# Attention in slots of six score steps instead of three, with GpSimd's queue in written order

## The chip, the cores and the metric

The kernel runs on one core of a Trainium2 chip. The metric is the device time of one execution in microseconds (us). Before the change the median of four runs is 950.72 us (950.05 to 951.18). PE is the matrix engine, DVE the vector engine, ACT the scalar engine, POOL is GpSimd, and SP is the engine that issues most DMAs here. SBUF is the on-chip memory, PSUM the banks into which the matrix engine writes.

## What is computed

Two blocks follow each other. The first is attention with a routing mask for 4 batches, 8 heads, 768 positions and 64 channels per head; a query sees only the keys whose nearest centroid (of 16 per head) is its own:

```python
mask = q_assign[:, :, :, None] == k_assign[:, :, None, :]
scores = scale * np.matmul(q, k.transpose(0, 1, 3, 2))
scores = np.where(mask, scores, -1000000000.0)
attn = np.exp(scores - np.max(scores, axis=-1, keepdims=True))
attn = attn / (np.sum(attn, axis=-1, keepdims=True) + 1e-09)
out = np.matmul(attn, v)
```

`q_assign` and `k_assign` are the argmax over the centroids of the normalized products. The second block takes the heads side by side as rows of 512, normalizes each row by its mean and variance, multiplies by `g_ln`, and adds `relu(xn @ w_ch1) @ w_ch2` (hidden width 2048) to the row. All is float32.

## The kernel before

**Tiling.** Two heads make a pair, so there are 16 pairs, numbered from 0. A pair is worked in two halves (384 queries each), and a half in six steps (128 keys each). One step (`scores`, line 380) is four groups of matmuls into one PSUM tile of two banks: the mask (two bf16 matmuls, one for each head) and the products of keys and queries (float32), and then one exp on ACT that writes a tile `e` of 128x768. There are three such PSUM tiles (`ps_s`), eight buffers for `e`, and one bank each for the sums (`ps_a`) and for everything else (`ps_t`). `weigh` (line 401) multiplies `e` by v on PE into the bank of `ps_a`, and DVE adds the `e` tiles of a half up into `es` for the denominators (lines 422 and 425, five additions a half). After the sixth step of a half ACT copies the sums into the tile `x` (line 434); `x` has two buffers, and a pair uses one.

**Preparation of the pair ahead.** `prep_transpose` turns q and k, either on PE in two groups of three with a copy on ACT each, or on DVE (line 280) when the load is in blocks of 32 columns. k of all pairs from 1 on is loaded in blocks, q of pair 1 and of the pairs from 7 on. `prep_sims` (295), `prep_turn` (314) and `prep_route` (323) find the nearest centroid, `prep_onehot` and `prep_mask` (339, 356) write three mask tiles on ACT.

**Finishing the pair behind** (`finish`, line 438). Part 0: the denominators by matmuls with ones (`den_ps`), a copy on ACT (`dsb`), and two small DMAs on POOL's queue, out to memory and back in another layout (`flat`, `rdens`). Part 1: a reciprocal on DVE (line 460) and three DMAs on POOL's queue (`row`, and two halves of `rb`). Part 2: `x` times `rb` on DVE (line 477) and a store. Part 3: a transpose on DVE (line 486) and four stores. Parts 0 and 1 of pair n-1 and parts 2 and 3 of pair n-2 run during pair n.

**Weights.** The weights come as 64-bit floats and are converted by six DVE instructions per chunk (`split_weight`, `join_weight`, lines 239 to 268), followed by a DMA on POOL's queue that adds the low part. The next chunk's load (line 236) goes out on SP when the one buffer is free. Pairs 0 to 6 convert two chunks, the later ones one.

**Work for the second block** of batch 0 is put into late pairs by `put` (lines 586 to 602): the row statistics (`norm_rows`, `norm_stats`, with a square root on ACT at line 524), `norm_stat_rows` (line 529: a transpose on PE, a copy on ACT, a store of 6 KB and two loads that spread mean and deviation over all partitions) and `norm_apply` (line 542), which subtracts and scales on DVE.

**Order.** The main loop (line 655) runs over four slots of three steps in each pair. In a slot PE computes the scores of the three steps after those that it weighs. PE, DVE and ACT execute in the order in which the loop writes their instructions; the order on SP and POOL is found by a planner. The second block (from line 721) gets its PSUM banks when the attention's pools are closed.

Of the kernel before, what the change touches and what calls it, by code (L numbers as in the profile page):

```python
# [8 lines left out]
F32 = mybir.dt.float32  # L9
# [10 lines left out]
def kernel(  # L20
# [11 lines left out]
    nc = tc.nc  # L32
# [37 lines left out]
    def ps(name, dt=F32, n=512):  # L70
        return pools["t"].tile([P, n], dt, tag="t", name=name)
# [201 lines left out]
    def prep_transpose(n, side, halves=range(NHALF)):  # L273
        src = loaded[n]["qk"[side]]
        if 0 in halves:
            prepared[n][side] = heads.tile([P, S], F32, tag=f"t{side}", name=f"t{side}")
        t_sb = prepared[n][side]
        if (n, "qk"[side]) in blocks:
            if 0 in halves:
                nc.vector.transpose(t_sb, src)  # L280
            return
        for g in halves:
# [7 lines left out]
            if n or side == 0 or g == 1:  # L290
# [147 lines left out]
    def finish(n, part):  # L438
        b, pr = pairs[n]
        if part == 0:  # L440
            den = ps("den_ps")
            for j in range(2):
                for g in range(NHALF):
                    r = (j * NHALF + g) * Q
                    nc.tensor.matmul(  # L445
                        den[r : r + Q, :HC], ones, sums[n, g][:, j, :],
                        start=True, stop=True, tile_position=(0, r),
                    )
            if n + 1 < len(pairs):
                dsb = last.tile([P, HC], F32, tag="dsb", name="dsb", bufs=1)  # L450
            else:
                dsb = late["all"][:, 1, :HC]
            nc.scalar.copy(dsb, den[:, :HC])
            flat = dram.tile([P // Q, HC], F32, tag="flat", name="flat")
            nc.gpsimd.dma_start(out=flat, in_=dsb[0:P:Q, :])
            nc.gpsimd.dma_start(
                out=rdens[:, n, :], in_=flat.rearrange("i (p e) -> (i p) e", e=DE)
            )
        elif part == 1:
            nc.vector.reciprocal(rdens[:, n, :], rdens[:, n, :])  # L460
# [13 lines left out]
            late[n] = rb  # L474
        elif part == 2:
            a, x = xs.pop(n), late[n]
            nc.vector.tensor_tensor(x, a, x, ALU.mult)
            nc.sync.dma_start(out=xT_d[b][pr], in_=x)
        else:
            x = late.pop(n)  # L480

            if n + 1 < len(pairs):
                y = last.tile([P, S], F32, tag="y", name="y")
            else:
                y = late["all"][:, 0]
# [41 lines left out]
        normed[b][1] = stat  # L527

    def norm_stat_rows(b):
        sp = ps("stat_ps")  # L530
        nc.tensor.transpose(
            sp[: 2 * NT, :P], normed[b][1].rearrange("p s t -> p (s t)"), ident
        )
        st = small.tile([2 * NT, P], F32, tag="st", name="st")
        nc.scalar.copy(st, sp[: 2 * NT, :P])
        nc.sync.dma_start(out=stat_d[b].rearrange("s (t p) -> (s t) p", p=P), in_=st)
        for i in range(2):
            row = xpool.tile([P, S], F32, tag="row", name="stat_row", bufs=2)
            nc.sync.dma_start(out=row, in_=stat_d[b][i : i + 1, :].to_broadcast([P, S]))
            normed[b].append(row)  # L540
# [51 lines left out]
    put(6, 2, rows_load, 0, 0)  # L592
# [7 lines left out]
    put(14, 1, x_sum, 0, 1)  # L600
    put(14, 3, x_sum, 0, 2)
    put(15, 2, w1_sums, 0, 0, (0, 1))


    steps = [(n, g, c) for n in range(len(pairs)) for g in range(NHALF) for c in range(NT)]
    per = NHALF * NT
    GROUP = 3
    slots = per // GROUP

    convert = {}  # L610
    for n in range(len(pairs)):
        for slot in (0, 2) if n < TWICE else (0,):
            convert[n, slot] = len(convert)
    order = {mybir.EngineType.PE, mybir.EngineType.DVE, mybir.EngineType.Activation}
    limit[0] = len(convert)
    with tc.manual_schedule(engines=order | {mybir.EngineType.SP}):
# [26 lines left out]
        prep_onehot(0)  # L643
        prep_mask(0, 0)
        prep_mask(0, 1)
        for i in range(1, GROUP):
            scores(i, "qk", ("qk",))
        for i in range(GROUP):
            scores(i, "qk", ("mask", "exp"))
        load_weight(0)  # L650
        for side in (1, 0):
            prep_transpose(1, side)
            load(2, "qk"[side])
    with tc.manual_schedule(engines=order):
        for u in range(len(pairs) * slots):
            n, slot = divmod(u, slots)
            nxt = n + 1 < len(pairs)
            if slot == 1:
                load(n + 1, "v")
            if slot == 1 and n > 1:  # L660
                finish(n - 2, 2)
            if slot == 1 and nxt:
                prep_sims(n + 1)
            if slot == 2 and nxt:
                prep_onehot(n + 1)
                prep_mask(n + 1, 0)
                prep_mask(n + 1, 1)
            if slot == 3 and n + 2 < len(pairs):
                prep_transpose(n + 2, 1)
                load(n + 3, "k")  # L670
                prep_transpose(n + 2, 0, (0,))
            for i in range(GROUP * (u + 1), min(GROUP * (u + 2), len(steps))):
                scores(i)
            if slot == 0 and n:
                finish(n - 1, 0)
            if slot == 1 and nxt:
                prep_turn(n + 1)
                prep_route(n + 1)
            if slot == 3 and n + 2 < len(pairs):
                prep_transpose(n + 2, 0, (1,))  # L680
                load(n + 3, "q")
            if slot == 1 and n > 1:
                finish(n - 2, 3)
            for i in range(GROUP * u, GROUP * (u + 1)):
                weigh(i)
            if slot == (2 if nxt else 1) and n:
                finish(n - 1, 1)
            if slot == 3 and not nxt:
                finish(n - 1, 2)
                finish(n - 1, 3)  # L690
# [479 lines left out]
```

## Time and profile before

| | us |
|---|---|
| median of four runs | 950.72 |
| the profiled execution's own time | 951.99 |
| its span | 950.2 |
| PE busy | 933.2 |
| DVE busy | 614.5 |
| ACT busy | 346.8 |
| POOL busy | 78.4 |

The attention fills about the first 361 us. The page of the profile gives the busy time of each engine, in tenths for 40 slices of the span, and groups of instructions by line with their mean duration and the idle time before them. The timeline gives single instructions with their start; what stands in brackets is the idle time of the engine before it and what ended it. A wait on an engine matters only where PE, or something that PE needs next, stands behind it.

### The profile page before, as it was taken

Reading aid. Unit: us, or ns where it says so; the run is one execution under the profiler, and the core shown is the slowest. Engines: PE = TensorE matmul, PEld = TensorE weight load, DVE = VectorE, ACT = ScalarE, POOL = GpSimd, SP = SyncE. Lnnn points to the kernel's source line nnn. Section 1 sums busy time; section 2 is a strip of 40 time slices with the busy share of each in tenths; the row PEclk is TensorE's granted clock in tenths of the full one; section 3 lists DMA queues with packets and bytes.
Section 4 is the critical chain, followed back from the end, with each engine's and each line's share of the span. In section 5 each row is a group of like instructions: output and inputs, shape, how many; then the busy total and the mean of one; then the engine's idle time right before and its main releaser. Section 6 shows DMA issues by size and latency. Waiting matters only on the chain.

```text
span 950.2 us, 12597 instructions
## 1 busy us (share of the span) xinstructions
PE 933.2 (98%) x4664; PEld 582.4 (61%) x4664; DVE 614.5 (65%) x1106; ACT 346.8 (36%) x554; POOL 78.4 (8%) x147
## 2 busy tenths in 40 slices
PE   8999999899999999999999999999999999999997
PEld 5444443344444444557887557887556887556886
DVE  5888888798999887898882446362436472344431
ACT  4667765477776762332001332001342000333000
POOL 2112111111111211110000000000000000000000
PEclk9999999999999999999999999999999999999999
DMA  6668898797798453664451002021002121000011
GB/s 141 150 150 196 190 195 182 158 193 159 173 166 147 112 132 99 147 140 141 140 155 39 0 1 78 22 95 40 1 0 65 36 84 50 1 1 7 29 45 36
DMA packets 179780, 92.48 MB, mean 97 GB/s; under 512 B 145792, under 2 KB 162288, under 8 KB 179712
## 3 DMA queue, kind: packets, MB, share of 16 engines
q1 hardware_dynamic: 170368, 76.20, 33.0%
q0 software_dynamic: 7744, 15.02, 8.0%
q8 instruction: 38, 0.62, 0.3%
q10 hardware_dynamic: 1600, 0.39, 0.2%
q14 instruction: 30, 0.25, 0.1%
HBM read 64.10 MB, written 19.10 MB: 88 GB/s over the span
## 4 chain that ended last, share of the span: by engine, by line
PE 83%; issue 7%; DVE 5%; DMA 2%; POOL 2%; ACT 0%; ACTq 0%; DVEq 0%; POOLq 0%
PE x_ps L831 17%; PE x_ps L738 16%; PE s_ps L396 11%; PE a_ps L408 9%; PE z_ps L831 9%; PE z_ps L738 8%; PE y_ps L831 4%; PE y_ps L738 4%; DMA row<-rdens 1%; DVE es L425 1%; PE sim_ps L302 1%; PE den_ps L445 1%; POOL w L268 1%; PE simT_ps L318 1%; PE oh_ps L344 1%
## 5 line engine op out<-in xcount | busy, mean ns | idle before, releaser
L391 ACT ACTIVATE e<-s_ps 128x768 f32<-128x768 f32 x192 | 150.2, 811 | 29.0 <-PE s_ps L396 24.1
L396 PE MATMUL s_ps<-t,t 64*128 64x384 f32 x768 | 155.2, 483 | 0.0
L408 PE MATMUL a_ps<-e,v_sb 128*64 128x384 f32 x768 | 138.8, 497 | 0.0
L425 DVE TENSOR_TENSOR es<-es,e 128x768 f32<-128x768 f32 x128 | 121.5, 949 | 10.7 <-ACT e L391 0.5
L408 PEld LDWEIGHTS a_ps<-e,v_sb 128*64 128x64 f32 x768 | 49.8, 137 | 75.4 <-issue 61.3
L758 DVE TENSOR_TENSOR h<-z_ps,u 128x384 f32<-128x384 f32 x64 | 35.6, 556 | 92.7 <-PE z_ps L738 71.3
L396 PEld LDWEIGHTS s_ps<-t,t 64*128 64x128 f32 x768 | 68.3, 188 | 28.6 <-issue 28.1
L831 PE MATMUL x_ps<-w2t,h 128*128 128x256 f32 x384 | 84.5, 379 | 0.0
L766 ACT ACTIVATE h<-h 128x384 f32<-128x384 f32 x96 | 49.9, 524 | 89.3 <-DVE h L758 89.3
L831 PEld LDWEIGHTS x_ps<-w2t,h 128*128 128x128 f32 x384 | 72.7, 190 | 10.1
L396 PE MATMUL s_ps<-m,mask 64*128 64x384 bf16 x192 | 62.4, 326 | 0.6 <-ACT e L391 0.6
L396 PE MATMUL s_ps<-mask,m 64*128 64x384 bf16 x192 | 62.2, 326 | 0.4 <-DVE mask L367 0.4
L753 ACT COPY u<-x_ps 128x384 f32<-128x384 f32 x64 | 30.7, 479 | 77.5 <-PE x_ps L738 77.5
L842 DVE TENSOR_TENSOR o_sb<-x_ps,xb 128x256 f32<-128x256 f32 x48 | 20.2, 420 | 50.4 <-PE x_ps L831 47.3
L753 ACT COPY p<-x_ps 128x384 f32<-128x384 f32 x32 | 15.0, 468 | 100.9 <-PE x_ps L738 97.4
L738 PE MATMUL x_ps<-xt,ws 128*128 128x384 f32 x128 | 46.7, 487 | 1.9 <-ACT p L753 1.1
L738 PE MATMUL x_ps<-xn,w 128*128 128x384 f32 x128 | 46.6, 487 | 0.6 <-ACT late L434 0.6
L738 PE MATMUL x_ps<-xn,ws 128*128 128x384 f32 x128 | 46.6, 487 | 0.2 <-DVE xn L567 0.2
L738 PE MATMUL z_ps<-xt,ws 128*128 128x384 f32 x128 | 46.6, 487 | 0.0
L738 PE MATMUL z_ps<-xn,ws 128*128 128x384 f32 x128 | 46.5, 486 | 0.0
L738 PE MATMUL x_ps<-xt,w 128*128 128x384 f32 x128 | 46.5, 486 | 0.0
L738 PE MATMUL y_ps<-xn,w 128*128 128x384 f32 x128 | 46.5, 486 | 0.0
(143 smaller groups left out, 1357.9 us busy)
## 6 DMA issues: line engine op xcount, KB each, us to landing
raw<-in_moe_w_ch_dram SPq DMA_DIRECT2D x32, 512.0 KB, 4.4
w<-tb POOLq DMA_DIRECT2D x32, 256.0 KB, 6.4
v_sb<-in_v_dram SPq DMA_DIRECT2D x32, 192.0 KB, 5.0
xn<-xT_d SPq DMA_DIRECT2D x16, 384.0 KB, 5.5
xr<-x_d SPq DMA_DIRECT2D x24, 256.0 KB, 3.1
xb<-x_d SPq DMA_DIRECT2D x48, 128.0 KB, 2.1
out_dram<-o_sb SPq DMA_DIRECT2D x48, 128.0 KB, 1.7
k_sb<-in_k_dram SPq DMA_DIRECT2D x62, 96.0 KB, 4.4
```

Source lines behind the costliest of these rows:

```text
L268: nc.gpsimd.dma_start(out=w, in_=fb, accum_op=ALU.add)
L302: nc.tensor.matmul(sim[r : r + Q, :HC], cT[:, pr, :, :].rearrange("p j c -> p (j c)"), prepared[n][side][:, g * HC : (g + 1) * HC], start= ...
L391: nc.scalar.activation(e, s[:, :, :HC], AF.Exp, scale=SCALE)
L396: nc.tensor.matmul(s[:, j, :HC], of_keys[:, keys], of_queries[:, cols], start=part == first, stop=part != first, skip_group_check=True,)
L408: nc.tensor.matmul(acc[j * D : (j + 1) * D, :HC], loaded[n]["v"][:, j, c, :], e[:, j, :], start=(c == 0), stop=(c == NT - 1),)
L425: nc.vector.tensor_tensor(es, es, soft.pop(i), ALU.add)
L738: nc.tensor.matmul(bank[:, :HC], lhs[:, c, :], rhs[:, c, :], start=first and c == 0, stop=c == NDH - 1, skip_group_check=True,)
L753: nc.scalar.copy(t, bank[:, :HC])
L758: nc.vector.tensor_tensor(h, bank[:, :HC], other, ALU.add)
L766: nc.scalar.activation(h, h, AF.Relu)
L831: nc.tensor.matmul(bank[:, :MH], hidden[lhs + (c,)][:, tt * P : (tt + 1) * P], rhs[:, c, :], start=first and c == 0, stop=c == NFH - 1, sk ...
L842: nc.vector.tensor_tensor(o, bank[:, :MH], x, ALU.add)
```

## The change

A slot now holds six steps, that is a half, and a pair has two slots. In a slot PE computes the scores of this half (`own`; the first three steps of pair 0 are done beforehand, `AHEAD`), then preparation, and then the products with v of the same half. Between scores and products stand `finish(n-1, 0)` and `prep_sims(n+1)` in slot 0, and `prep_onehot`, `prep_mask` and the PE transposes of q in slot 1. The transposes of q use a `ps_s` tile, six at a time with one copy; the denominators use the bank of `ps_a`. The conversion of a chunk is written before the half's `weigh`, in both slots of pairs 0 to 6 and in slot 0 of the later ones. After `weigh` come, in slot 0, `finish(n-2, 2)` and `(n-2, 3)` and the routing of pair n+1, and in slot 1 `finish(n-1, 1)` and the DVE transposes of k and q. The `put` jobs move to the two slots; `norm_stat_rows` goes into a new place between scores and products of slot 1 of pair 10. POOL's instructions keep the written order too. In pair 15 `finish(14, 0)` is written ahead of the scores, and `finish(15, 0)` ahead of the second block's first products.

```diff
@@ prep_transpose
+        if n:
+            t = ps_s.tile([P, 2, 512], F32, tag="s", name="qk_ps")
+            for c in range(NT):
+                nc.tensor.transpose(
...
+            nc.scalar.copy(t_sb.rearrange("p (g c) -> p g c", g=NHALF), t[:, :, :HC])
+            return
         for g in halves:
-            t = ps("qk_ps") if n else ps_s.tile([P, 2, 512], F32, tag="s", name="qk_ps")[:, 0]
+            t = ps_s.tile([P, 2, 512], F32, tag="s", name="qk_ps")[:, 0]
...
@@ finish, part 0
-            den = ps("den_ps")
+            den = ps_a.tile([P, 512], F32, tag="a", name="den_ps") if n + 1 < len(pairs) else ps("den_ps")
...
@@ norm_stat_rows
-        sp = ps("stat_ps")
+        sp = ps("stat_ps") if b else ps_s.tile([P, 2, 512], F32, tag="s", name="stat_ps")[:, 0]
...
-        put(7 + t // 2, (0, 2)[t % 2], norm_rows, 0, t)
-    put(9, 2, norm_stats, 0)
-    put(9, 3, norm_stat_rows, 0)
+        put(7 + t // 2, t % 2, norm_rows, 0, t)
+    put(9, 1, norm_stats, 0)
+    put(10, "between", norm_stat_rows, 0)
     for i in range(2):
         for c in range(NDC):
-            put(10 + 2 * i + c // 2, 2, norm_apply, 0, i, c)
+            put(10 + 2 * i + c // 2, 1 if i == 0 else c % 2, norm_apply, 0, i, c)
...
-    GROUP = 3
+    GROUP = NT
+    AHEAD = 3
...
-    with tc.manual_schedule(engines=order):
+    with tc.manual_schedule(engines=order | {mybir.EngineType.Pool}):
...
+            own = range(GROUP * u, GROUP * (u + 1))
+            if slot == 0 and not nxt:
+                finish(n - 1, 0)
+            for i in own:
+                if i >= AHEAD:
+                    scores(i)
+            if slot == 0:
+                if n and nxt:
+                    finish(n - 1, 0)
+                if nxt:
+                    prep_sims(n + 1)
+            elif nxt:
                 prep_onehot(n + 1)
                 prep_mask(n + 1, 0)
                 prep_mask(n + 1, 1)
...
+                if n + 2 < len(pairs) and (n + 2, "q") not in blocks:
+                    prep_transpose(n + 2, 0)
+                    load(n + 3, "q")
+            for job in extra.pop((n, "between"), ()) if slot else ():
+                job()
             if (n, slot) in convert:
                 m = convert[n, slot]
                 split_weight(m)
                 join_weight(m)
                 load_weight(m + 1)
+            for i in own:
+                weigh(i)
+            if slot == 0:
+                load(n + 1, "v")
+                if n > 1:
+                    finish(n - 2, 2)
+                    finish(n - 2, 3)
+                if nxt:
+                    prep_turn(n + 1)
+                    prep_route(n + 1)
+                else:
+                    finish(n - 1, 1)
+            elif not nxt:
+                for part in (2, 3):
+                    finish(n - 1, part)
+            else:
+                if n:
+                    finish(n - 1, 1)
+                if n + 2 < len(pairs):
+                    for side in (1, 0):
+                        if (n + 2, "qk"[side]) in blocks:
+                            prep_transpose(n + 2, side)
+                            load(n + 3, "qk"[side])
             for job in extra.pop((n, slot), ()):
                 job()
...
     with tc.manual_schedule(engines=order):
+        finish(len(pairs) - 1, 0)
         first_layer(0, 0, 1)
         first_layer(0, 0, 2)
         first_layer(0, 0, 6)
-        finish(len(pairs) - 1, 0)
```

More of the change, by code (lines that the diff above doesn't have):

```diff
@@ L281, in prep_transpose @@
             return
+        if n:
+            t = ps_s.tile([P, 2, 512], F32, tag="s", name="qk_ps")
+            for c in range(NT):
+                nc.tensor.transpose(
+                    t[:, c // TH, c % TH * P : (c % TH + 1) * P],
+                    src[:, c, :, :].rearrange("p h d -> p (h d)"),
+                    ident,
+                )
+            nc.scalar.copy(t_sb.rearrange("p (g c) -> p g c", g=NHALF), t[:, :, :HC])
+            return
         for g in halves:
-            t = ps("qk_ps") if n else ps_s.tile([P, 2, 512], F32, tag="s", name="qk_ps")[:, 0]
+            t = ps_s.tile([P, 2, 512], F32, tag="s", name="qk_ps")[:, 0]
             for c in range(TH):
@@ L289, in prep_transpose @@
                 )
-            if n or side == 0 or g == 1:
+            if side == 0 or g == 1:
                 nc.scalar.copy(t_sb[:, g * HC : (g + 1) * HC], t[:, :HC])
@@ L591 @@
     put(6, 0, norm_load, 0)
-    put(6, 2, rows_load, 0, 0)
+    put(6, 1, rows_load, 0, 0)
     for t in range(NT):
-        put(7 + t // 2, (0, 2)[t % 2], norm_rows, 0, t)
-    put(9, 2, norm_stats, 0)
-    put(9, 3, norm_stat_rows, 0)
+        put(7 + t // 2, t % 2, norm_rows, 0, t)
+    put(9, 1, norm_stats, 0)
+    put(10, "between", norm_stat_rows, 0)
     for i in range(2):
         for c in range(NDC):
-            put(10 + 2 * i + c // 2, 2, norm_apply, 0, i, c)
-    put(14, 1, x_sum, 0, 1)
-    put(14, 3, x_sum, 0, 2)
-    put(15, 2, w1_sums, 0, 0, (0, 1))
+            put(10 + 2 * i + c // 2, 1 if i == 0 else c % 2, norm_apply, 0, i, c)
+    put(14, 0, x_sum, 0, 1)
+    put(14, 1, x_sum, 0, 2)
+    put(15, 1, w1_sums, 0, 0, (0, 1))
     steps = [(n, g, c) for n in range(len(pairs)) for g in range(NHALF) for c in range(NT)]
     per = NHALF * NT
-    GROUP = 3
+    GROUP = NT
+    AHEAD = 3
     slots = per // GROUP
@@ L611 @@
     for n in range(len(pairs)):
-        for slot in (0, 2) if n < TWICE else (0,):
+        for slot in (0, 1) if n < TWICE else (0,):
             convert[n, slot] = len(convert)
@@ L645 @@
         prep_mask(0, 1)
-        for i in range(1, GROUP):
+        for i in range(1, AHEAD):
             scores(i, "qk", ("qk",))
-        for i in range(GROUP):
+        for i in range(AHEAD):
             scores(i, "qk", ("mask", "exp"))
@@ L657 @@
             nxt = n + 1 < len(pairs)
[L658 to L664, printed above, removed]
+            own = range(GROUP * u, GROUP * (u + 1))
[10 more added lines that the diff above has]
+            elif nxt:
                 prep_onehot(n + 1)
@@ L667 @@
                 prep_mask(n + 1, 1)
[L668 to L690, printed above, removed]
+                if n + 2 < len(pairs) and (n + 2, "q") not in blocks:
[3 more added lines that the diff above has]
+                job()
             if (n, slot) in convert:
```

## The prediction

> **What bounds the kernel now.** I read the page's slices first, then the timeline of PE, and then DVE, ACT and SP at the places where PE waits.
>
> ```profile
> PE   8999999899999999999999999999999999999997
> DVE  5888888798999887898882446362436472344431
> ```
>
> PE is busy nearly everywhere, so a gain must shorten PE's own sequence or remove one of its few waits. In the attention (the first 15 slices or so) DVE is close behind. The timeline of PE, at the last pair:
>
> ```profile
> 352.16 2.16 PE L408 MATMUL a_ps<-e,v_sb 128*64 128x384 f32 x12
> 354.25 0.33 PE L396 MATMUL s_ps<-m,mask 64*128 64x384 bf16 x1
> ...
> 355.07 0.32 PE L396 MATMUL s_ps<-m,mask 64*128 64x384 bf16 x1
> ...
> 355.87 0.32 PE L396 MATMUL s_ps<-m,mask 64*128 64x384 bf16 x1
> ...
> 356.77 4.09 PE L408 MATMUL a_ps<-e,v_sb 128*64 128x384 f32 x24
> 361.44 1.56 PE L738 MATMUL x_ps<-xn,w 128*128 128x384 f32 x4 [0.58 <-ACT late L434]
> 362.84 1.45 PE L738 MATMUL y_ps<-xn,w 128*128 128x384 f32 x4
> 365.36 1.56 PE L738 MATMUL x_ps<-xt,ws 128*128 128x384 f32 x4 [1.07 <-ACT p L753]
> ```
>
> Starts give what a group costs PE. A score step takes 0.82 or 0.80, the third 0.90 because the kind changes behind it; three steps 2.52. Three steps of products take 2.09 (352.16 to 354.25). Two such groups in a row, seen here only at the end, last 4.09, not 2.09 + 2.16. PE's waits in the attention are these:
>
> ```profile
> 151.54 0.85 PE L445 MATMUL den_ps<-es,ones 128*32 128x384 f32 x6 [2.33 <-DVE es L425]
> ...
> 177.39 1.50 PE L445 MATMUL den_ps<-es,ones 128*32 128x384 f32 x6 [4.08 <-DVE es L425]
> 178.82 3.14 PE L408 MATMUL a_ps<-e,v_sb 128*64 128x384 f32 x12
> ```
>
> The denominators of pairs 5 and 6 wait for DVE's additions, and DVE had waited for a small DMA:
>
> ```profile
> 143.28 0.23 DVE L460 RECIPROCAL rdens<-rdens 128x12 f32<-128x12 f32 x1 [2.14 <-DMA rdens<-flat]
> ...
> 169.13 0.23 DVE L460 RECIPROCAL rdens<-rdens 128x12 f32<-128x12 f32 x1 [3.89 <-DMA rdens<-flat]
> ```
>
> After the longer wait PE runs slower for a while (1.50 for six instead of 0.85 for eight, 3.14 instead of 2.16).
>
> **What the change takes away.** (a) 31 joints between score groups at 0.90 - 0.81 = 0.09 and 31 between product groups at 4.25 - 4.09 = 0.16: 7.7. (b) Five times two groups of three transposes of q become one of six: about 0.1 each, 0.5. (c) The waits above. From one pair's first denominator matmul to the next it is 20.94 in undisturbed pairs, and 21.50, 24.10 and 27.49 in pairs 5, 6 and 7: 10.3 too much. In POOL's old order `flat` stood behind a weight DMA that waited for DVE (issued 157.60 after 157.03, long after `dsb`); in written order it goes first. (d) At the end, 1.07 and 0.19 for an `rb` that landed late: now a half earlier, 1.3. Sum 19.8.
>
> **The new order, laid out.** Let T be the time from a pair's first score matmul. PE without waits: six scores to 4.97, denominators 0.78, similarities 0.79, six products 4.02 (to 10.56), turn 0.48, six scores from 11.04 to 16.01, one-hot 0.44, six products to 20.47; 0.87 more where q is turned on PE. The first exp starts 1.03 after the first score and takes 0.81. With three score tiles, the fourth score step (T = 13.49 in slot 1) needs the first exp's end.
>
> DVE, with a lag L behind the pair's start: conversion 3.31, five additions 4.89, so the product with `rb` (0.95) ends at L + 9.15; transpose 0.9, routing 1.08 (needs the turn, T = 11.1); in slot 1 conversion 3.31, additions 4.89, reciprocal 0.2, k and q 0.9 each. That is 20.5 for pairs 1 to 4, where PE needs 21.3, and 21.4 for pairs 5 and 6, where PE needs 20.5.
>
> Here is a new wait. Before, the product with `rb` was written ahead of ACT's copy of the first half's sums into `x`, 268.8 against 271.85. Now it is written behind, and `x` has two buffers, so the copy of pair n waits for the product of pair n-2. All exps of slot 1 stand behind that copy on ACT, and PE's fourth score step behind the first exp: L + 9.15 + 0.1 + 0.48 + 0.81 = L + 10.6 against 13.49. PE loses L - 2.9 whenever L is above 2.9.
>
> **What it adds.**
> - Pairs 5 to 8. L is near 0.1 to 1 up to pair 4. From then q too is loaded in blocks; SP needs 8.6 to 10.2 for the eight block loads (147.69 to 156.34; 124.45 to 134.72), and the next chunk's raw load, which must land for slot 1's conversion at T = 12.3, goes out behind them and takes 4.4. It lands 12.4 to 14.4. So pairs 5 and 6 add 0.9 of work each and 0 to 2 of waiting: L is 2.5 to 4.3 at pair 6 and 4.3 to 5.7 at pair 7, PE loses 0 to 1.4 and 1.4 to 2.8. I take 3.0. Bounds: nothing, if the loads are quick; 9, if `rb` lands in 8.5, its longest, not in its median 4.4.
> - The square root after pair 9.
>
> ```profile
> 235.53 1.28 ACT L524 ACT_TABLE_LOAD   x1
> 236.82 0.30 ACT L524 ACTIVATE stat<-mv,eps 128x6 f32<-128x6 f32 x1
> 237.14 1.28 ACT L391 ACT_TABLE_LOAD   x1
> ...
> 240.88 0.25 ACT L535 COPY st<-stat_ps 12x128 f32<-12x128 f32 x1
> ```
>
> These take 2.9 from 235.53 to 238.43, hidden before by the three steps that PE had in hand. Now they start when the pair's last sums are copied (T = 21.1), the first exp ends at 24.8 and PE wanted it at 22.9: 1.9. Bounds 0 and 2.9.
> - The row statistics in pair 10. `norm_stat_rows` moves from the end of pair 9 to slot 1 of pair 10, and the first `norm_apply` stays in that slot: DVE meets it about 10 us sooner. On ACT the copy `st` stands behind three masks (3.0) and ends 0.5 before the products do. SP then:
>
> ```profile
> 238.34 2.90 SPq L86 DMA_DIRECT2D k_sb<-in_k_dram  x4
> 241.34 2.71 SPq L86 DMA_DIRECT2D q_sb<-in_q_dram  x4
> 244.15 0.62 SPq L536 DMA_DIRECT2D stat_d<-st  x1
> ...
> 248.21 0.86 SPq L539 DMA_DIRECT2D stat_row<-stat_d  x2
> ```
>
> Before, the store left 3.0 after `st` (241.13), behind k and q, and the same loads stand there now. In a later batch with a free queue store to load is 2.4 (617.68 to 620.11), and the rows land 4.5 after issue. I take 3.0 + 2.4 + 4.5 = 9.9; then two subtractions of 0.9, less the 0.5: L = 11.2 at pair 11, and PE loses 8.3, plus 1.8 for the slow stretch after a long idle (1.50 - 0.64 and 3.14 - 2.16 above): 10.1. Bounds: free queue, 6.0 from copy to first subtraction (617.66 to 623.65), 6.2 in all; old spacing 7.1 and the longest landing 7.7, 15.
> - Pair 15: the denominators of pair 14 come first and wait for the bank's copy, 0.1 + 0.48 + 0.07 = 0.65.
> - Starting: similarities of pair 1 come 2 us earlier than before, and DVE's transposes may be late: 0.3 (0 to 2).
> - Each slot 0: products wait for `dsb`, ready at 6.4 to 6.5 against 6.54; 0.05 times 14 = 0.7 (0 to 1.5).
>
> POOL: `flat` goes at T = 6.5 and lands in 4.4, `rdens` follows and lands in 3.0, so at about 15 for a reciprocal at 20.5; by the longest rows (7.8 and 7.6) at 22.6, 2 late. The weight DMA behind them waits some 6 us longer; its buffer is next needed half a pair after it lands. The w additions of slot 1 now precede `row`, which costs `rb` about 1.
>
> Sum of what is added: 3.0 + 1.9 + 10.1 + 0.65 + 0.3 + 0.7 = 16.7. Against 19.8 that leaves -3.1 on the profiled execution's own 951.99 (span 950.2 and 1.8 around it), which stands 1.3 above the median: 947.6 on the median's scale.
>
> Two rules of the Trainium skill would move single terms. "DMA: Bandwidth & Descriptors", Latency and other measured facts, gives a fixed cost of about 2 us per DMA; by it the two DMAs of the row statistics would take 4 us instead of 9.9 and the estimate would be near 940, but even the trace's free queue shows 6.0. "ScalarE: Activation LUTs", What ACT_TABLE_LOAD costs, gives 2.66 us for each switch of table sets, 5.3 for two; by it the wait at the square root would be 4.6 and the estimate 950.3, but the trace's pair of loads with the square root between took 2.9.
>
> **Rivals.**
> - Short waits. If statistics arrive as with a free queue (6.2) and pairs 5 to 8 lose 1: 19.8 - 10.8 = 9.0, so 941.7. For it: the planner may put the store ahead of k and q. Against: `st` ends after DVE has released k and q.
> - DVE's lag feeds on itself (slower). Place: the product with `rb` in front of ACT's copy, from pair 2 on. DVE has 0.9 to spare per pair up to pair 4 and lacks 0.9 in pairs 5 and 6. If raw loads and `rb` together cost DVE 2.5 a pair, L grows 1.6 a pair, passes 2.9 at pair 4, and PE pays the growth from there: 1.6, 3.4, 3.4 and in pair 7 again 1.6, 10.0 instead of my 3.0: 954.6. It decides from 0.9 of waiting a pair. For it: DMAs are busy for 0.9 of the time in this stage. Against: DVE waited for no raw load in the attention.
> - The joints save nothing, because without steps in hand each group of products starts late by what the joint saved: 7.7 less, 955.3. Against: products start 1.2 after the last score, behind other work, and need only the first exp.
>
> **How the numbers follow.** Forecast 0.46, its own range 943 to 952; short waits 0.14; the lag 0.28; no saving 0.12. No change that a measurement of this kernel can tell is within 0.2%, 1.9 us. Faster: 0.37 of the forecast, all of the short waits; same: 0.09 of the forecast and 0.03 of the last; the rest is slower. From 940 to 960 leaves out about 0.16.
>
> **What would show it.** Score groups of 4.97 and product groups of 4.02 from start to start; undisturbed pairs at 20.5; `rdens` with no wait; ACT's copy into `x` waiting for DVE's product in pairs 6, 7 and 11; a DVE wait of some 8 us for `stat_row` near 250, and PE idle about 8 behind it. It would be wrong if DVE lags already in pairs 2 to 4, or if SP's new order holds a load that I took as early.

## The result, and the profile after

The changed kernel takes 952.04 us (median; 947.5 to 955.23), the kernel before 951.29 in the same series; the ratio is 1.0006, 95% interval 0.9999 to 1.0013. That is no change that can be told. The forecast, 947.6, was 4.4 too low; the measured time lies at the upper edge of its range, 943 to 952. The spans of the two profiled executions, 950.1 and 950.2, agree with this, but hardly a part of the attention takes the time it took before: some 23 us were gained and about as much lost.

Where the time went shows first in the busy tenths of the slices (page of the changed kernel). The twelfth slice is a new hole in PE, with the clock granted to PE lower there as well, and DVE has one in the eleventh; the shorter waits further ahead don't take a slice of 23.8 below nine tenths:

```profile
PE   8999999999969999999999999999999999999997
...
DVE  5998889999599987799792446372435472344431
...
PEclk9999999999979999999999999999999999999999
```

What was gained is in the timeline of PE. This is pair 2, from its first score matmul to that of pair 3 (start, duration, line, names, shapes):

```profile
54.33 0.33 PE L406 MATMUL s_ps<-m,mask 64*128 64x384 bf16 x1
...
59.28 0.85 PE L455 MATMUL den_ps<-es,ones 128*32 128x384 f32 x8
...
60.73 4.09 PE L418 MATMUL a_ps<-e,v_sb 128*64 128x384 f32 x24
...
65.23 0.33 PE L406 MATMUL s_ps<-m,mask 64*128 64x384 bf16 x1
...
70.18 0.51 PE L354 MATMUL oh_ps<-identb,onehot 128*128 128x128 bf16 x6
70.53 0.82 PE L285 MATMUL qk_ps<-ident,q_sb 128*128 128x128 f32 x6
71.28 4.09 PE L418 MATMUL a_ps<-e,v_sb 128*64 128x384 f32 x24
75.30 0.33 PE L406 MATMUL s_ps<-m,mask 64*128 64x384 bf16 x1
```

Six scores take 4.95 from start to start, six products 4.02, and the whole pair 20.97, where it took 21.90 before. A pair without transposes of q on PE takes 20.31 instead of 20.94. The den waits of pairs 5 to 7 are gone: nothing idles ahead of `den_ps` until pair 15.

What was lost is mostly one kind of wait, PE's score steps waiting for an exp. In the view of waits (waiting instruction, releaser: total, times, longest) it is the largest of PE's, and the largest of ACT's in the attention (0 to 364) stands behind it:

```profile
PE s_ps L406 <- ACT e L401: 18.3, 8, 7.7
...
ACT x L444 <- DVE rb L487: 58.5, 9, 13.0
```

The timelines show the whole chain, from PE back to ACT's copy into `x` and on to DVE's product, at pairs 3, 4 and 11 (idle time and releaser in brackets). First PE:

```profile
90.80 0.32 PE L406 MATMUL s_ps<-m,mask 64*128 64x384 bf16 x1 [2.00 <-ACT e L401]
...
114.16 0.48 PE L406 MATMUL s_ps<-m,mask 64*128 64x384 bf16 x1 [2.21 <-ACT e L401]
...
273.15 0.48 PE L406 MATMUL s_ps<-m,mask 64*128 64x384 bf16 x1 [7.69 <-ACT e L401]
...
274.70 0.52 PE L406 MATMUL s_ps<-m,mask 64*128 64x384 bf16 x1
```

Then ACT:

```profile
89.56 0.48 ACT L444 COPY x<-a_ps 128x384 f32<-128x384 f32 x1 [7.26 <-DVE rb L487]
...
112.92 0.48 ACT L444 COPY x<-a_ps 128x384 f32<-128x384 f32 x1 [7.47 <-DVE rb L487]
...
271.90 0.48 ACT L444 COPY x<-a_ps 128x384 f32<-128x384 f32 x1 [12.95 <-DVE rb L487]
```

And DVE, which in pairs 3 to 5 waits for `rb` to land (the third is put down to a load of v that lands at the same time) and in pair 10 for the spread rows:

```profile
88.51 0.96 DVE L487 TENSOR_TENSOR rb<-x,rb 128x768 f32<-128x768 f32 x1 [2.65 <-DMA rb<-row]
...
111.87 0.96 DVE L487 TENSOR_TENSOR rb<-x,rb 128x768 f32<-128x768 f32 x1 [2.51 <-DMA rb<-row]
...
135.97 0.96 DVE L487 TENSOR_TENSOR rb<-x,rb 128x768 f32<-128x768 f32 x1 [3.27 <-DMA v_sb<-in_v_dram]
...
260.68 1.83 DVE L556 TENSOR_TENSOR xn<-xn,stat_row 128x768 f32<-128x768 f32 x2 [8.46 <-DMA stat_row<-stat_d]
```

The loss in each pair is read from one pair's first denominator matmul to the next's, less the undisturbed 20.98 (20.31 from pair 5 on). It is larger than the idle time where PE runs slower after a long wait: in pair 11 a step of scores takes 1.55 (273.15 to 274.70) instead of 0.81, and the clock granted between 272 and 276 is 0.50. The same reading for all runs is the table that the experiments refer to (us; "root" is the wait at the square root in pair 10's first half; column 14 holds pair 15 too, with 16.01 and 19.38 as the undisturbed values; the pairs without a column lose 0 to 0.6; the attention's end is the start of the last denominators):

| kernel | pair 3 | 4 | 5 | 6 | 7 | root | 11 | 14 | end of attention | time | ratio to before |
|---|---|---|---|---|---|---|---|---|---|---|---|
| changed | 2.2 | 4.0 | 1.5 | 1.3 | 1.8 | 2.0 | 10.2 | 0 | 363.5 | 952.0 | 1.0006 |
| pool_planned | 2.8 | 2.7 | 1.8 | 1.3 | 3.9 | 2.0 | 8.4 | 0 | 364.4 | 953.9 | 1.0010 |
| x3 | 0.1 | 3.1 | 1.8 | 1.3 | 2.9 | 4.7 | 7.0 | 0 | 362.1 | 952.9 | 1.0005 |
| recip_early | 0 | 0.2 | 1.0 | 1.4 | 2.5 | 4.1 | 7.5 | 0 | 358.7 | 946.5 | 0.9926 |
| x3_recip | 0 | 0 | 0 | 0.1 | 2.6 | 6.2 | 7.2 | 0 | 358.5 | 946.9 | 0.9941 |
| conv_moved | 0 | 1.3 | 1.9 | 1.3 | 1.7 | 2.0 | 8.1 | 3.9 | 361.1 | 951.8 | 0.9990 |
| lean | 1.2 | 0.7 | 4.0 | 0 | 0.1 | 2.0 | 8.7 | 0 | 358.3 | 947.8 | 0.9971 |
| no_add | 0 | 0 | 2.0 | 1.3 | 1.3 | 2.2 | 8.8 | 0 | 357.0 | 945.1 | 0.9934 |
| apply11 | 2.5 | 4.0 | 0.8 | 1.4 | 2.0 | 2.0 | 0 | 0 | 353.7 | 944.5 | 0.9914 |
| four | 0 | 0 | 0 | 0 | 1.6 | 0.9 | 0 | 4.8 | 348.6 | 937.4 | 0.9832 |
| four_x3 | 0 | 0 | 0 | 0 | 0 | 0.9 | 0 | 2.7 | 344.9 | 933.7 | 0.9804 |
| best | 0 | 0 | 0 | 0 | 0 | 0.9 | 0 | 0 | 340.7 | 930.7 | 0.9784 |

The start, up to the first denominators, differs by up to 1.3 between these executions (38.30 to 39.58); the last columns hold that too.

### The profile page after: what moved, and what is told of

The parts are those of the page before. It is cut to its first block, busy times and chain, and to the rows that moved or that the text cites. A ratio compares the mean times of both kernels' runs of the same rounds, so it can differ in the third digit from the quotient of the medians.

```text
span 950.1 us, 12611 instructions
## 1 busy us (share of the span) xinstructions
PE 922.4 (97%) x4664; PEld 590.7 (62%) x4664; DVE 617.9 (65%) x1106; ACT 346.0 (36%) x549; POOL 79.1 (8%) x147
## 4 chain that ended last, share of the span: by engine, by line
PE 80%; DVE 11%; DMA 6%; issue 2%; ACT 1%; DVEq 0%; POOL 0%; SPq 0%; ACTq 0%; POOLq 0%
PE x_ps L853 17%; PE x_ps L760 16%; PE s_ps L406 10%; PE z_ps L853 9%; PE z_ps L760 8%; PE a_ps L418 8%; PE y_ps L853 4%; PE y_ps L760 4%; DVE es L435 3%; DMA rb<-row 1%; DMA v_sb<-in_v_dram 1%; DVE w L260 1%; DVE tb L265 1%; DVE ta L248 1%; DMA q_sb<-in_q_dram 1%
## 5 line engine op out<-in xcount | busy, mean ns | idle before, releaser
L406 PE MATMUL s_ps<-t,t 64*128 64x384 f32 x768 | 158.7, 492 | 0.0
L418 PE MATMUL a_ps<-e,v_sb 128*64 128x384 f32 x768 | 130.9, 490 | 0.0
L418 PEld LDWEIGHTS a_ps<-e,v_sb 128*64 128x64 f32 x768 | 52.3, 137 | 70.0 <-issue 58.2
L853 PEld LDWEIGHTS x_ps<-w2t,h 128*128 128x128 f32 x384 | 72.7, 190 | 10.1
L444 ACT COPY x<-a_ps 128x384 f32<-128x384 f32 x30 | 14.3, 478 | 91.2 <-DVE rb L487 58.5
```

What stands on the lines that cost most here:

```text
L406: nc.tensor.matmul(s[:, j, :HC], of_keys[:, keys], of_queries[:, cols], start=part == first, stop=part != first, skip_group_check=True,)
L418: nc.tensor.matmul(acc[j * D : (j + 1) * D, :HC], loaded[n]["v"][:, j, c, :], e[:, j, :], start=(c == 0), stop=(c == NT - 1),)
L444: nc.scalar.copy(xs[n][:, g * HC : (g + 1) * HC], accs.pop((n, g))[:, :HC])
L853: nc.tensor.matmul(bank[:, :MH], hidden[lhs + (c,)][:, tt * P : (tt + 1) * P], rhs[:, c, :], start=first and c == 0, stop=c == NFH - 1, sk ...
```

## The experiments

**Is it the two buffers of x?** The edit writes the transposed result over `x` and gives the room of `y` to a third buffer.

```diff
-                    xs[n] = last.tile([P, S], F32, tag="x", name="x", bufs=2)
+                    xs[n] = last.tile([P, S], F32, tag="x", name="x", bufs=3)
...
-            a, x = xs.pop(n), late[n]
+            a, x = xs[n], late[n]
...
-            if n + 1 < len(pairs):
-                y = last.tile([P, S], F32, tag="y", name="y")
-            else:
-                y = late["all"][:, 0]
+            y = xs.pop(n)
```

> One edit to the changed kernel: x gets three buffers instead of two; the space is found by writing the transposed result over x and dropping the tile y. Theory: the two buffers of x, with the product with rb now written late, make PE wait in slot 1 of pairs 3 to 7 (2.18 + 4.05 + 1.47 + 1.31 + 1.75 = 10.8) and in pair 11 (10.25). With a third buffer the copy of pair n needs the product of pair n-3: the five waits go, and of pair 11's some 4 go, since DVE still stands 8.5 for the statistics and the one-hot of the next pair comes behind it. Sum 14 to 15 less than the changed kernel, about 937. Rival: DVE is full (20.8 of work against 20.97 for a pair on PE), and x is only the first place where its lag shows; then the wait passes on to the e buffers, the denominators or the one-hot, and less than 3 is gained, 948 or more.

Measured: 952.85, ratio 1.0005 (0.9988 to 1.0021), so nothing that the times can tell. The copies into `x` no longer wait for DVE, but PE now waits for the one-hot of the next pair, which DVE makes three instructions behind the product with `rb`. PE in this kernel, pairs 4 to 6:

```profile
116.06 0.51 PE L354 MATMUL oh_ps<-identb,onehot 128*128 128x128 bf16 x6 [3.06 <-DVE onehot L339]
...
138.80 0.51 PE L354 MATMUL oh_ps<-identb,onehot 128*128 128x128 bf16 x6 [1.70 <-DVE onehot L339]
...
160.42 0.51 PE L354 MATMUL oh_ps<-identb,onehot 128*128 128x128 bf16 x6 [1.05 <-DVE onehot L339]
```

The theory fell, the rival stood: the two buffers are where DVE's lag shows first, not what causes it. And the lateness that PE no longer waits out in pairs 3 and 11 shows elsewhere: the wait at the square root grew from 2.0 to 4.7, because DVE finishes the last row statistics late, and ACT's square root waits for them.

**The spread rows in pair 11.** Edit:

```diff
-            put(10 + 2 * i + c // 2, 1 if i == 0 else c % 2, norm_apply, 0, i, c)
+            put(11 + i + c // 2, c % 2, norm_apply, 0, i, c)
```

> One edit to the changed kernel: the four subtractions of norm_apply go to pairs 11 and 12 and the four products with the deviation to pairs 12 and 13, so that DVE meets the spread rows a pair later. Theory: DVE's 8.5 for stat_row near 252 is the whole cause of the 10.25 in slot 1 of pair 11; it goes, and the time is 10 less than the changed kernel's, 942. Rival: the rows land so late because SP's queue and the DMAs are full there, and what DVE no longer waits for comes back as a wait for k, q or rb in pairs 11 and 12, or the four additional instructions in pair 12 make DVE late there; then 5 or less is gained, 947 or more.

Measured: 944.54, ratio 0.9914 (0.9884 to 0.9944). The time lies between the theory's and the rival's, but the timeline is on the theory's side: the wait of 10.2 is gone, 0.5 in pairs 12 and 13 is all that came in its place, and the attention ends 9.8 earlier; of PE's waits in the stage only the one at the square root is left in this timeline (226 to 300):

```profile
233.97 0.32 PE L406 MATMUL s_ps<-m,mask 64*128 64x384 bf16 x1 [1.78 <-ACT e L401]
```

**The reciprocal earlier.** Edit (the later call is left out for these pairs):

```diff
+            early = slot == 1 and 0 < n < TWICE
+            if early:
+                finish(n - 1, 1)
             for i in own:
                 weigh(i)
```

> One edit to the changed kernel: in pairs 1 to 6 the reciprocal and the three DMAs behind it (row, rb) are written ahead of the additions of slot 1 instead of behind them, 5 earlier on DVE. Theory: DVE has no time to spare up to pair 6, and its waits for rb in the product (2.65, 2.51, 3.27) are what makes it late in pairs 3 to 5; rb lands 5 earlier and is there in time, so the waits of 2.18 and 4.05 in pairs 3 and 4 go and those of pairs 5 to 7 (4.5) shrink to 0 to 2: 8 to 10 less than the changed kernel, 942 to 944. Rival: POOL in written order or the DMAs hold rb back whenever the reciprocal is done (6.7 from rb's issue to its landing), or DVE now stands waiting for rdens; then 3 or less is gained.

Measured: 946.53, ratio 0.9926 (0.9897 to 0.9956), between the theory's 944 and the rival's 949. In pairs 3 to 7 the waits fell from 10.8 to 5.1, and in pair 11 by 2.8, but at the square root 2.1 came back. DVE's waits for `rb` in its product shrank to these:

```profile
87.12 0.96 DVE L487 TENSOR_TENSOR rb<-x,rb 128x768 f32<-128x768 f32 x1 [0.93 <-DMA rb<-row]
...
108.76 0.96 DVE L487 TENSOR_TENSOR rb<-x,rb 128x768 f32<-128x768 f32 x1 [0.51 <-DMA rb<-row]
...
130.73 0.96 DVE L487 TENSOR_TENSOR rb<-x,rb 128x768 f32<-128x768 f32 x1 [1.15 <-DMA rb<-row]
```

The theory had them vanish, and they didn't. `row` was issued at 72.56 instead of 76.92, but `rb` could only follow at 80.23 instead of 81.68, so most of the 4.4 was lost while the 6 KB of `row` landed (the trace puts POOL's wait of 6.79 there down to a load of q that lands at the same time). That asked for the run without weight DMAs below.

**POOL's written order on the kernel before.** Edit:

```diff
-    with tc.manual_schedule(engines=order):
+    with tc.manual_schedule(engines=order | {mybir.EngineType.Pool}):
         for u in range(len(pairs) * slots):
```

> One edit to the kernel before: POOL's queue in written order, nothing else. Theory of the prediction, term (c): the waits of den_ps in pairs 5, 6 and 7 (10.3 in all) come from flat standing behind a weight DMA in the planner's order; in written order they go, 951.3 - 10.3 = 941, and then most of what the change gained was to be had from this one word. Rival: they come from DVE, which has more work than PE in these pairs, and the order on POOL only decides where it shows; then 948 or more. A written order can also put row or flat behind a weight DMA elsewhere and cost as much as it gives: 951 to 955.

Measured: 941.90, ratio 0.9882 (0.9854 to 0.9910). The theory held. `flat` now goes ahead of the weight DMA, and nothing idles ahead of the denominators of pair 5 or 6. POOL in this kernel, and PE:

```profile
150.57 0.64 POOL L455 DMA_DIRECT2D flat<-dsb  x1 [3.34 <-ACT dsb L453]
155.24 0.59 POOL L456 DMA_DIRECT2D rdens<-flat  x1 [4.03 <-DMA flat<-dsb]
155.83 0.91 POOL L268 DMA_DIRECT2D w<-tb  x1
```

```profile
147.96 1.78 PE L445 MATMUL den_ps<-es,ones 128*32 128x384 f32 x8
...
169.83 1.78 PE L445 MATMUL den_ps<-es,ones 128*32 128x384 f32 x8
```

Each of these still takes 0.93 longer than the usual 0.85, so 8.4 of the 10.3 went; another 1.3 came at the end, where `rb` of pair 14 was early too. One word of the change, alone, is worth more than the whole.

**The slots without that word.** The changed kernel, with the order on POOL left to the planner (`engines=order`):

> The change without its last part: slots of six as changed, the order on POOL left to the planner. Theory: the change is two changes of opposite sign, POOL's written order (10.7 less, as it gave alone on the kernel before) and the slots (10 to 11 more, since the new waits of 23.0 and 1.3 outweigh 13 of joints and transposes); the slots alone then take 958 to 963. Rival: written order holds rb back in the new arrangement (row waits on POOL for nothing but stands behind a weight DMA), so that the planner's order is as good or better here: 948 to 953.

Measured: 953.89, ratio 1.0010 (0.9995 to 1.0026), the same as the changed kernel. The two parts don't add up: with the slots, the planner still puts `flat` behind a weight DMA (at 83.80, 108.04, 131.93), but the reciprocal stands half a pair later, and DVE never waits for `rdens`. So the time, 0.9 above the rival's range, is far nearer to the rival than to the theory, though not for the rival's reason: the written order does no harm and no good here.

**Less work on DVE.** Two runs. The first moves a conversion from pair 2 to pair 13:

```diff
-        for slot in (0, 1) if n < TWICE else (0,):
+        for slot in (0, 1) if n < TWICE and n != 2 or n == 13 else (0,):
```

> One edit to the changed kernel: the second conversion of pair 2 (3.4 on DVE) goes to pair 13, where DVE has time to spare; the 23 chunks stay. Theory: DVE's lag, and not x or POOL, is what PE waits for; with 3.4 less of work before it, DVE is 3.4 earlier from pair 3 on, and the waits of pairs 3 to 7 (10.8) go but for 1 or 2 in pair 4 or 5, where rb, 5 behind the reciprocal, still sets the product: 8 to 10 less than the changed kernel, 942 to 944. Rival: rb lands late by its own DMAs, DVE only waits longer for it in pairs 3 to 5 and loses the 3.4 again: 3 or less gained, 949 or more.

Measured: 951.80, ratio 0.9990 (0.9980 to 0.9999). Of 10.8 in pairs 3 to 7, 6.2 stayed, and pair 14, right behind the work that pair 13 inherited, lost 3.9: DVE had no time to spare there. The second leaves two of the six instructions out in every conversion of pairs 1 to 6, so these weights are not the right ones:

```diff
-        nc.vector.scalar_tensor_tensor(
+        if not 2 <= m < 14:
+          nc.vector.scalar_tensor_tensor(
             out=ta, in0=hi, scalar=0xC0000000, in1=ta, op0=ALU.bitwise_and, op1=ALU.bitwise_or
         )
...
-        nc.vector.tensor_single_scalar(tb, w.bitcast(U32), 0xFF800000, op=ALU.bitwise_and)
+        if not 2 <= m < 14:
+          nc.vector.tensor_single_scalar(tb, w.bitcast(U32), 0xFF800000, op=ALU.bitwise_and)
```

> The changed kernel with two of the six DVE instructions left out in each conversion of pairs 1 to 6 (the one that sets the high bits of ta, 0.69, and the masking of tb, 0.43), so that these chunks of the weights are wrong: 2.2 less work for DVE in each of these pairs, everything else, x and the order of rb included, as in the changed kernel. Theory: the waits in pairs 3 to 7 (10.8) are DVE's want of time; with 18.6 of work a pair against 21.0 it catches up what it loses to rb, and 1 or less of the waits is left: 941 to 943. Rival: rb's path from the reciprocal (row, rb, 12 to 13 in all) sets the waits in pairs 3 to 5 by itself: 5 to 6 of the waits stay there, and the time is 946 to 948.

Measured: 947.79, ratio 0.9971 (0.9948 to 0.9994). Pairs 6 and 7 lost their waits, pairs 3 to 5 kept 6.0. There DVE turned its free time into waits for DMAs, for `rb` and now for the raw weights too:

```profile
88.63 0.96 DVE L489 TENSOR_TENSOR rb<-x,rb 128x768 f32<-128x768 f32 x1 [3.83 <-DMA rb<-row]
...
124.20 0.43 DVE L245 TENSOR_SCALAR ta<-raw 128x512 uint32<-128x512 uint32 x1 [2.59 <-DMA raw<-in_moe_w_ch_dram]
...
133.64 0.96 DVE L489 TENSOR_TENSOR rb<-x,rb 128x768 f32<-128x768 f32 x1 [2.11 <-DMA rb<-row]
```

So the rival held for pairs 3 to 5 and the theory for 6 and 7: two causes.

**Fuller or emptier DMAs.** The windows of the changed kernel (stretch, then busy time of PE, PEld, DVE, ACT and POOL, and at the end the clock, the busy share of the DMA engines and GB/s) show full DMA engines where `row` and `rb` are under way in pair 3 (in pair 4 it is 0.98 and 1.04, from 97 to 102 and from 102 to 107), and half-empty ones where the same `row` is in pair 6:

```profile
75.00:80.00 5.00, 5.00 (x40) 2.62 (x36) 4.79 (x9) 4.04 (x7) 0.57 (x1) 1.00 1.07 243
...
145.00:150.00 5.00, 5.00 (x39) 2.62 (x36) 4.76 (x8) 4.07 (x6) 0.71 (x2) 1.00 0.49 114
```

POOL in the changed kernel waits accordingly for `row` before it issues `rb`; the weight DMA written ahead of both is shown too:

```profile
71.66 0.86 POOL L268 DMA_DIRECT2D w<-tb  x1 [3.20 <-DVE tb L265]
76.92 0.57 POOL L472 DMA_DIRECT2D row<-rdens  x1 [4.39 <-DVE rdens L470]
81.68 1.08 POOL L480 DMA_DIRECT2D rb<-row  x2 [4.19 <-DMA row<-rdens]
...
142.62 0.86 POOL L268 DMA_DIRECT2D w<-tb  x1 [4.43 <-DVE tb L265]
147.87 0.57 POOL L472 DMA_DIRECT2D row<-rdens  x1 [4.39 <-DVE rdens L470]
149.87 1.07 POOL L480 DMA_DIRECT2D rb<-row  x2 [1.42 <-DMA row<-rdens]
```

The edit takes the weight DMAs of pairs 1 to 6 away, two in each pair:

```diff
-        nc.gpsimd.dma_start(out=w, in_=fb, accum_op=ALU.add)
+        if not 2 <= m < 14:
+            nc.gpsimd.dma_start(out=w, in_=fb, accum_op=ALU.add)
```

> The changed kernel without the 12 DMAs on POOL's queue that add the low part of the weights in pairs 1 to 6 (256 KB each), so that these weights keep their high part alone. DVE's work, the written order and x stay. In the changed kernel row, a store of 6 KB, takes 4.1 and rb 6 to 7 around 75 to 85 and 97 to 107, where the DMA engines are busy for 0.98 to 1.07 of the time, and row takes 2.0 around 148, where they are at 0.49. Theory: full DMA engines make rb late; with 512 KB a pair less, rb lands 2 to 3 sooner, DVE's waits of 2.65, 2.51 and 3.27 go to 0 to 1, and the waits in pairs 3 to 5 fall from 7.7 to 1 to 3: 947 to 949. Rival: the two steps behind the reciprocal take what they take whatever else is moved, or the loads fill the room: pairs 3 to 5 keep 6 or more, 951 to 953.

Measured: 945.14, ratio 0.9934 (0.9914 to 0.9953). The waits of pairs 3 and 4 are gone, and 2.0 is left in pair 5. POOL in this kernel:

```profile
77.81 0.55 POOL L473 DMA_DIRECT2D row<-rdens  x1 [9.38 <-DVE rdens L471]
80.02 1.05 POOL L481 DMA_DIRECT2D rb<-row  x2 [1.66 <-DMA row<-rdens]
...
119.29 0.55 POOL L473 DMA_DIRECT2D row<-rdens  x1 [8.41 <-DVE rdens L471]
123.14 1.06 POOL L481 DMA_DIRECT2D rb<-row  x2 [3.30 <-DMA row<-rdens]
```

`row` lands in time in pair 3, and in pair 5, where it is slow (3.30 on POOL), DVE waits 3.0 and PE 2.0. What makes DVE wait for `rb` in pairs 3 and 4 is thus the weight DMAs; which of a pair's two was not told apart. Does `row` stand behind the nearer one in POOL's queue, or share the DMA engines with it? In the changed kernel that one goes out 5.3 ahead of `row` in pair 3 and in pair 6 alike, and is still under way when `row` follows: it lands 7.0 and 6.2 after its own issue. Yet `row` takes 4.1 to land in pair 3 and 1.7 in pair 6, as little as in pair 3 without weight DMAs. The DMA engines were busy for 1.10 of the time while `row` was under way in pair 3 (76.9 to 81.1) and for 0.08 in pair 6 (147.9 to 149.3), and for 0.61 in the slow pair 5 without weight DMAs (119.3 to 122.6). That speaks for the engines, but no run changed one of the two alone.

**Together.** First the third buffer and the early reciprocal:

> The third buffer for x and the early reciprocal together. The third buffer alone gave nothing, since DVE's lag then held the one-hot; the early reciprocal alone gave 6 and left 5.2 of waits in pairs 4 to 7. Theory: what counts is DVE's lag alone, so the third buffer takes 2 at most from these: 943 to 946. Rival: once DVE waits less for rb the copy into x binds again by itself and its buffer is worth 4 or more, as it was with the other four edits (3.7): 942 or less.

Measured: 946.93, ratio 0.9941 (0.9914 to 0.9967), no less than the early reciprocal alone, and above what either the theory or the rival had. In pairs 4 to 7 the waits fell from 5.1 to 2.7, and the square root took that back, 6.2 instead of 4.1. ACT there loads a table and then waits for DVE, with all exps behind it:

```profile
223.47 1.28 ACT L531 ACT_TABLE_LOAD   x1
226.58 0.30 ACT L531 ACTIVATE stat<-mv,eps 128x6 f32<-128x6 f32 x1 [1.82 <-DVE mv L525]
226.90 1.28 ACT L401 ACT_TABLE_LOAD   x1
```

Then four edits at once: `norm_apply` as in apply11, the early reciprocal, the moved conversion, and the square root between scores and products of the first half of pair 10, with its two DVE instructions written behind those products:

```diff
...
-    put(9, 1, norm_stats, 0)
+    put(10, "turned", norm_stats, 0)
+    put(10, 0, norm_stats, 0, 1)
...
-            for job in extra.pop((n, "between"), ()) if slot else ():
+            for job in extra.pop((n, "between" if slot else "turned"), ()):
```

> Four edits to the changed kernel together: subtractions and products of norm_apply a pair later, the reciprocal of pairs 1 to 6 ahead of the additions, one conversion moved from pair 2 to pair 13, and the square root on ACT put between scores and products of slot 0 of pair 10, with its two DVE instructions behind the products. Theory: with DVE no longer late, none of the waits of the changed kernel is left but 0 to 3 in pairs 5 to 7 and 1.3 at the end: 952 - 23 + 1.5 = 930, range 928 to 934; that is 11 below the kernel before with POOL in written order, the worth of the joints. Rival: DVE and PE are both near full, and each wait taken away comes back in the next pair: 936 to 941, no better than the kernel before with POOL's order alone.

Measured: 937.39, ratio 0.9832 (0.9809 to 0.9854): a time in the rival's range, but not for its reason. Pairs 1 to 6 and most others ran at 20.98 and 20.31 without a wait, and none came back in the next pair; the miss is pair 14 (4.8), to which DVE comes late behind the conversion moved to pair 13, and pair 7 (1.6). With the third buffer as a fifth edit:

> The four edits and a third buffer for x (y dropped) as a fifth. Theory: where DVE is in time, x has no part in any wait: the same as the four within 1. If instead the two buffers still bind in pairs 5 to 7, 2 to 3 less. The other way about, the exps that no longer stand behind the copy change nothing, since the one-hot needs the same DVE 2 later: 0.

Measured: 933.67, ratio 0.9804 (0.9785 to 0.9822); by the medians 3.7 less than the four where 0 to 1 was expected, by the timelines in pairs 7 (1.6), 13 (0.5) and 14 (2.2). A buffer is worth something where DVE is late for a moment and nothing where it is late for good. Last, the conversion in pair 15 instead of 13, and the denominators of pair 14 in the bank of `ps_t`:

```diff
-        for slot in (0, 1) if n < TWICE else (0,):
+        for slot in (0, 1) if n < TWICE and n != 2 or n == 15 else (0,):
...
-            den = ps_a.tile([P, 512], F32, tag="a", name="den_ps") if n + 1 < len(pairs) else ps("den_ps")
+            den = ps_a.tile([P, 512], F32, tag="a", name="den_ps") if n + 2 < len(pairs) else ps("den_ps")
```

> The five edits with two places changed: the moved conversion goes to slot 1 of pair 15, where DVE stands idle for 5 to 6, instead of pair 13, and the denominators of pair 14 use the bank of ps_t, so that they need not wait for the copy of the sums. Theory: pair 14's waits (1.7 and 0.9) go, and 0.7 of the wait ahead of the denominators; DVE is 2 late in pair 15, which costs up to 0.5: 933.7 - 2.8 = 931, range 930 to 932.5. Rival: the late conversion holds the first layer's subtractions and the last denominators, and 2 or more comes back: 933 or more.

Measured: 930.68, ratio 0.9784 (0.9764 to 0.9805), as the theory had it, and better than both kernels. Of PE's waits these are the largest left (view of waits):

```profile
PE s_ps L406 <- ACT e L401: 1.2, 2, 0.6
```

By the medians it is 11.2 below the kernel before with POOL in written order, by the ratios 9.3; the joints are worth 10.6 by the count below, and here the slots finally pay.

## Why the prediction was right or wrong

- **Joints and transposes of q**: put at 8.2, measured 10.6 (four pairs at 0.92, eleven at 0.63). What was missed: the denominators in front of the similarities take 0.67 from start to start, not 0.78, and the transposes 0.75 for all six. That the joints save nothing, the third rival, is refuted by every undisturbed pair.
- **The den waits of pairs 5 to 7**: put at 10.3 and gone. Their cause as told, `flat` behind a weight DMA in the planner's order, is shown by the kernel before with POOL in written order (8.4 of 10.3).
- **The end**: 1.3 of waits for a late `rb` gone, as put.
- **The copy into x waiting for the product with rb**: the mechanism was seen, with its place, in pairs 3 to 7 and 11 of the timeline, and so was its size: with L as measured (2.1, 2.4, 0.8, 3.9 and 4.4 in pairs 3 to 7) and DVE's wait for `rb` (2.65, 2.51, 3.27, 0 and 0), their sum less 2.9 gives 1.8, 2.0, 1.1, 1.0 and 1.5, and PE idled 2.0, 2.2, 1.3, 1.1 and 1.6. It is the path by which DVE's lag reaches PE and not the cause of the loss: a third buffer moved the wait to the one-hot and saved nothing.
- **Pairs 3 and 4**: put at 0, measured 6.2. This is the step that failed. It said that L is near 0.1 to 1 up to pair 4. DVE's conversion begins 4.4 after the first score in pair 1, 2.3 in pair 2 and 2.1 in pair 3 (54.33 and 75.30 are the first scores of pairs 2 and 3):

```profile
33.35 0.33 PE L406 MATMUL s_ps<-m,mask 64*128 64x384 bf16 x1
...
37.72 0.39 DVE L245 TENSOR_SCALAR ta<-raw 128x512 uint32<-128x512 uint32 x1
...
56.62 0.40 DVE L245 TENSOR_SCALAR ta<-raw 128x512 uint32<-128x512 uint32 x1
...
77.38 0.38 DVE L245 TENSOR_SCALAR ta<-raw 128x512 uint32<-128x512 uint32 x1
```

  The start leaves DVE late, and with 20.8 of work in a pair of 20.98 (56.62 to 77.38, without a gap) it can't catch up. With L at 2.1 and 2.4 in pairs 3 and 4, most of its waits for `rb`, 2.65 and 2.51, reaches PE, as 2.0 and 2.2, and behind the second PE's score steps stand 1.6 apart (114.16, 115.72 and 117.31) instead of 0.81. The prediction named this sign itself, a DVE that lags already in pairs 2 to 4. And the wait for `rb` was sized wrong: "the w additions of slot 1 now precede `row`, which costs `rb` about 1". Without them POOL waits 1.66 instead of 4.19 for `row` in pair 3, 1.43 instead of 4.14 in pair 4, and PE not at all.
- **Pairs 5 to 8**: put at 3.0 (0 to 9), measured 4.5. The second rival, a lag that feeds on itself, gave 10.0 for pairs 4 to 7, where 8.6 were measured, and 10.8 with pair 3; for this term it was the better forecast. Its point of decision, 0.9 of waiting a pair, was passed by the 2.5 to 3.3 that DVE waited in pairs 3 to 5.
- **The square root**: put at 1.9, measured 2.0. The Trainium skill, "ScalarE: Activation LUTs", What ACT_TABLE_LOAD costs, gives 2.66 us a switch, and an estimate from it would have been 4.6. In the trace the two loads take 1.28 each and, with the square root between, 2.9 from 230.19 to 233.08; the measurement decides.
- **Row statistics in pair 10**: put at 10.1, measured 10.2, with DVE's wait of 8.5 as foretold. That the sum was right is partly luck, for its parts weren't: the store left at 252.08, 0.5 after the copy and not 3.0, and then DVE could start only 6.4 after the two loads were issued (254.31), not 4.5. The Trainium skill, "DMA: Bandwidth & Descriptors", Latency and other measured facts, gives a fixed cost of about 2 us per DMA, and an estimate from it would have been 4 for the two steps. The trace shows 8.6 from the store's issue to DVE's start.
- **Pair 15**: 0.65, as put. **Start**: put at 0.3 lost, 1.0 gained in these two executions (39.28 and 38.30), within what it varies. **dsb**: put at 0.7, nothing seen.

Gains 10.6 + 10.3 + 1.3 + 1.0 = 23.2 against the 19.8 forecast; losses 6.2 + 4.5 + 2.0 + 10.2 + 0.65 = 23.6 against 16.7. Each side came out larger, the losses by more, and what was left was nothing instead of 3.1. That the forecast missed by only 4.4 is luck in part: the gains it missed made up for half of the losses it missed.

## What to carry to other kernels

When an engine off the critical path has 20.8 of work in a period of 21.0, its slack is already spent: count where it stands at the start, and charge its DMA waits to the bound engine, less the little that is left. A buffer added where the wait shows only moved the wait here, to the next thing that engine makes; take the lateness away at its source, and look for what the freed lateness does further on. And try the parts of a change alone: here POOL's order alone gave 1.2%, the slots alone nothing, both together nothing, and the slots with their waits mended 2.2%.

## What was not expected of the hardware

A store of 6 KB and the DMAs that read it back held up a kernel that moves 92 MB: POOL waited 4.1 to 4.6 for `row` to land in pairs 3 to 5, 1.4 in pair 6 and 7.7 passed from its issue to that of `rb` ahead of pair 3's product in the run with the early reciprocal, where it went out right behind a weight DMA and the DMA engines were busy for 0.96 to 1.09 of the time (72 to 82). Issuing it 4.4 earlier made `rb` 1.4 earlier.
